# Fused attention and gated feed-forward: six single PSUM banks for the slots of batches 2 to 7

## The chip, the cores and the metric

The kernel runs on one core of a Trainium2 chip. The metric is the device time of one execution in microseconds (us). The names in the text: PE is TensorE (matrix products, and the weight loads PEld ahead of them), DVE is VectorE, ACT is ScalarE, POOL is GpSimd, SP is SyncE, which issues transfers. A bank is one of the eight pieces of PSUM, the memory that PE writes to; a bank holds 512 fp32 numbers in each of 128 partitions.

## The reference

```
def sm_attn(qq, kk, vv):
    s = scale * qq @ kk.T                  # per batch and head
    a = exp(s - max(s)); a = a / (sum(a) + 1e-9)
    return a @ vv
p_packed = sm_attn(p, k, v)                # 32 packed rows per head
out = sm_attn(q, p_packed, p_packed)       # 576 tokens per head
x = out as [8 * 576 tokens, 8 heads * 64]
h = x @ w_in                               # 512 -> 2048
g = h * cos(h)
result = g @ w_out                         # 2048 -> 512, fp32
```

There are 8 batches, 8 heads, 576 tokens, head size 64; the feed-forward part has 4608 rows, 512 inputs and 2048 hidden columns.

## The kernel before, in words

Everything is bf16 on PE, with fp32 in PSUM. The order on every engine is the order in which the code is written (`manual_schedule`); buffers only decide which earlier instruction a new one must wait for.

The second attention's product and w_in are merged: `ppw` multiplies the packed rows with w_in once per batch (PPW, in four quarters n = 0 to 3 of 512 columns), and h is then a2n (the normalised second attention weights, 256 rows in two halves y = 0, 1, 576 tokens) times PPW. The stages of batch s:

- `s2(s)`: 16 score products (L143) from ppT and q; ACT takes their exponentials into a2u.
- `sums2(s, y)`: PE sums each half with a block of ones (L239); ACT takes the logarithm (L241).
- `normalise(s)`: ACT takes exp(-log) for both halves (L247), then DVE multiplies a2u, the reciprocal of the first sums and that into a2n, first half 0, then half 1 (L249).
- `slot(s)`: 16 steps fc = 0 to 15, one for each 128 hidden columns. `h_mm` makes h for all 576 tokens in a pair of banks, 288 columns in each: two products with half 0 of a2n and two with half 1 (L263). ACT takes the cosine (L267, a sine with a bias), DVE the product h * cos(h) into gT (L270). After steps 7 and 15 POOL copies the last 64 tokens of eight steps into `joint` (L274), where two batches share 128 rows.
- Inside the slot, after step 7, `tiled` runs `ppw` quarters 2 and 3 (L213) and the packed rows `pp` of the next batch (L186), which are written into columns that h leaves unused in step 7's second bank (`spare`). After step 15's products `pp_T` (L198) transposes the packed rows of the next batch.

PE's gaps are filled with output products: `out_gen` gives, one at a time, the 128x512 products g @ w_out of the batch before (L351; 4 or 5 chunks of 16, accumulated in the two banks of the pool O, copied out by ACT or DVE and stored by SP), and `fill(n)` issues n of them. `slot` spreads those left over its steps, except for `keep`, which are left for later; `heavy={7: (5, 4)}` gives step 7 more, the last 4 of them behind its hook.

Besides O's two banks there are six. `banks(pairs)` closes the pool and opens it anew: `banks(3)` has three pairs (`psa`), `banks(0)` six single banks (`one`). Batch 0 runs its h with single banks, 512 tokens at a time (`h_one`), and its last 64 tokens follow in batch 1's slot at once (`h_rest`, L303); from batch 1 on there are three pairs.

PE's order in the stage of batch 4 (S scores, p8 the eight products of one `ppw`, Z the two of `sums2`, o an output product, H4 the four of a step, pp and T those of `pp` and `pp_T`):

```
S16 p8 o8 S16(first scores of batch 5) p8 o4 Z2 o5 Z2 o13
H4 o1 H4 o2 H4 o2 H4 o2 H4 o1 H4 o2 H4 o2 H4 o6 p16 pp48 o4
H4 o2 H4 o2 H4 o2 H4 o1 H4 o2 H4 o2 H4 o2 H4 T2 o7
```

Of the kernel before, what the change touches and what calls it, by code (L numbers as in the profile page):

```python
# [9 lines left out]
BF16 = mybir.dt.bfloat16  # L10
# [5 lines left out]
def kernel(  # L16
# [90 lines left out]
    def pe_T(n, b, engs=(V, V, V), groups=(0, 1, 2), own=None):  # L107
        if 0 in groups:
            xT[n, b] = att_pool.tile([128, H * 3, TP], BF16, name=n + "T", tag=n + "T", bufs=2 if n == "k" else 1)
        t = xT[n, b]  # L110
        flat = bf[n, b].rearrange("p h x -> p (h x)")
        for i in groups:
            ps = own(BF16) if own else psa(BF16)[:, 0, :]
            for j in range(8):
                o = 8 * i + j
                nc.tensor.transpose(ps[:, j * TP:(j + 1) * TP], flat[:, o * 128:(o + 1) * 128],  # L116
                                    ident[0:TP, 0:TP])
            to = t[:, 8 * i:8 * i + 8].rearrange("p a x -> p (a x)"), ps[:, 0:8 * TP]
            if engs[i] is None:
                return to  # L120
            copy(engs[i], *to)

    def bank(dt=FP32):
        return O.tile([128, 512 if dt == FP32 else 1024], dt, name="ot", tag="ot")
# [54 lines left out]
    def pp(b, eng=V, own=None):  # L179

        ps = own() if own else psa()[:, 0, :]
        for y in range(2):
            for j in range(C):
                c = 2 * (j % 3) + j // 3
                for x in range(4):
                    nc.tensor.matmul(ps[32 * x:32 * x + 32, y * D:(y + 1) * D],  # L186
                                     a1T[b][0:TP, y, j, 32 * x:32 * x + 32],
                                     bf["v", b][:, 2 * x + y, c * D:(c + 1) * D],
                                     start=(j == 0), stop=(j == C - 1))
        t = pp_sb[b % 2].rearrange("p a d -> p (a d)")  # L190
        copy(eng, t[:, 0:2 * D], ps[:, 0:2 * D])
        copy(eng, t[:, 2 * D:3 * D], ps[:, 0:D])
# [5 lines left out]
            nc.tensor.transpose(ps[:, i * 128:(i + 1) * 128], t[:, i * D:i * D + 128], ident)  # L198
        copy(eng, ppT[b % 2].rearrange("p i x n -> p (i x n)"), ps[:, 0:256])

    def ppw(b, n, eng=None, own=False, later=False, cuts=((0, 512),)):
        if b not in PPW:
            PPW[b] = ppw_pool.tile([128, 2, DF], BF16, name="PPW", tag="PPW")
        two = isinstance(eng, tuple)
        if own:
            ps = [bank(), bank()]
        else:
            t = psa()
            ps = [t[:, 0, :], t[:, 1, :]]
        for x in range(4):  # L210
            for y in range(2):
                r = slice(64 * y, 64 * y + 64)
                nc.tensor.matmul(ps[y][32 * x:32 * x + 32, :], ppT[b % 2][r, 0, x, :],  # L213
                                 w_in_bf[r, x, n * 512:(n + 1) * 512], start=True, stop=True)

        def evacuate(cuts=cuts):
            if own or two:
                for a, z in cuts:
                    for y in range(2):
                        copy(eng[y] if two else eng, PPW[b][:, y, n * 512 + a:n * 512 + z], ps[y][:, a:z])  # L220
            else:
                copy(eng or (V, ACT)[n % 2], PPW[b][:, :, n * 512:(n + 1) * 512], t)
        if later:
            return [lambda c=c: evacuate((c,)) for c in cuts]
        evacuate()
# [25 lines left out]

    gT, joint = {}, {}

    spare = [None]

    def h_mm(b, fc):
        if fc == 0:
            g_tile(b)
        ps = psa()
        spare[0] = ps[:, 1, HS:512]  # L260
        for y in range(2):
            for e in range(2):
                nc.tensor.matmul(ps[:, e, 0:HS], PPW[b][:, y, fc * 128:(fc + 1) * 128],  # L263
                                 a2n[b][:, y, e * HS:(e + 1) * HS], start=(y == 0), stop=(y == 1))
        cs = cos_pool.tile([128, S], BF16, name="cosT")
        csv = cs.rearrange("p (e x) -> p e x", e=2)
        ACT.activation(out=csv, in_=ps[:, :, 0:HS], func=AF.Sin, bias=PI_HALF)  # L267

        def rest():
            V.tensor_tensor(out=gT[b][:, fc, :].rearrange("p (e x) -> p e x", e=2),  # L270
                            in0=ps[:, :, 0:HS], in1=csv, op=ALU.mult)
            if fc % 8 == 7:
                j0 = (b % 2) * 64
                G.tensor_copy(out=joint[b // 2][:, fc - 7:fc + 1, j0:j0 + 64],  # L274
                              in_=gT[b][:, fc - 7:fc + 1, 512:576])
        return rest
# [21 lines left out]
    def h_rest(b):  # L298

        t = psa()  # L300
        for fc in range(NFC):
            for y in range(2):
                nc.tensor.matmul(t[:, fc // 8, (fc % 8) * 64:(fc % 8) * 64 + 64],  # L303
                                 PPW[b][:, y, fc * 128:(fc + 1) * 128], a2n[b][:, y, 512:576],
                                 start=(y == 0), stop=(y == 1))
        cs = cos_pool.tile([128, 2, 512], BF16, name="cosR", bufs=1)
        ACT.activation(out=cs, in_=t, func=AF.Sin, bias=PI_HALF)
        j0 = (b % 2) * 64
        V.tensor_tensor(out=joint[b // 2][:, :, j0:j0 + 64],
                        in0=t.rearrange("p a (f x) -> p (a f) x", x=64),  # L310
                        in1=cs.rearrange("p a (f x) -> p (a f) x", x=64), op=ALU.mult)

    osb_eng = [V]

# [50 lines left out]
    def to_do():  # L365
        return sum(n for _, n in filler)
# [73 lines left out]
    normalise(0)  # L440
    s1(1)
    ACT.preload_act_table_set(SIN_SET)
    cut_ppw, rest_ppw = ppw(0, 0, V, own=True, later=True, cuts=((0, 128), (128, 512)))
    warm(3, psa()[:, 0, :])
    cut_ppw()
    rest_ppw()
# [3 lines left out]
    for fc in range(13):  # L450
        h_one(0, fc)()()
        if fc in (0, 4, 8):
            ppw(0, 1 + fc // 4, (ACT, ACT if fc == 8 else V), own=True)
    c13 = h_one(0, 13)
    pp(1, ACT, own=bank)
    c13()()
# [27 lines left out]
    rest_ppw()  # L484
    fill(7)

    def slot(s, hooks, keep=0, heavy={}, last=None):


        left = to_do() - keep  # L490
        weight = [1 + heavy.get(fc, (0, 0))[0] for fc in range(NFC)]
        for fc in range(NFC):
            rest = h_mm(s, fc)
            if fc == NFC - 1 and last:
                last()
            rest()
            quota = (left * sum(weight[:fc + 1])) // sum(weight) - (left + keep - to_do())
            behind = min(quota, heavy[fc][1]) if fc in heavy else quota
            fill(quota - behind)
            while hooks and hooks[0][0] == fc:  # L500
                hooks.pop(0)[1]()
            fill(behind)
# [5 lines left out]
    def tiled(b):  # L508


        own, later = spare[0], []
        for n in (2, 3):
            later += ppw(b, n, (ACT, V)[n - 2], later=True)
        later[0]()
        pp(b + 1, V, own=lambda: own)
        later[1]()

    def tk2():
# [8 lines left out]
    def cross(n, b):  # L527
        return lambda: xbar(n, b)

    osb_eng[0] = ACT  # L530
    slot(1, [(2, lambda: pw2(1, 2, (ACT, V))), (4, lambda: h_rest(0)), (6, lambda: pack_p(2, 4)), (7, cross("k", 3)),
             (8, tk2), (9, cross("q", 2)), (10, lambda: pe_T("k", 2, (V, V, ACT), (2,)))], 4, {2: (1, 2), 4: (3, 5)})
    ACT.preload_act_table_set(EXP_SET)
    osb_eng[0] = V
    behind(xT["q", 2][0:1, 0, 0:1])
# [36 lines left out]
        load(n, b)  # L572
    fill(9)
    osb_eng[0] = ACT
    slot(2, [(7, lambda: tiled(2))], 10, {7: (5, 4)}, lambda: pp_T(3, V))

    for s in range(3, B):
        nxt = s + 1 < B
        ACT.preload_act_table_set(EXP_SET)
        osb_eng[0] = V  # L580
        set_filler(s - 1)
        fill(5)
        s2(s)
        ppw(s, 0, V)
        fill(8 if nxt else 9)
        if nxt:
            s1(s + 1)
            ppw(s, 1, V)
            a1_xbar(s + 1)
            xbar("q", s + 1)  # L590
            recips(s + 1)
            if s + 2 < B:
                xbar("k", s + 2)
                behind(xT["k", s + 2][0:1, 0, 0:1])
        else:
            for n in range(1, 4):
                ppw(s, n, V)
        fill(4 if nxt else 5)
        sums2(s, 0)
        fill(5)  # L600
        sums2(s, 1)
        normalise(s)
        ACT.preload_act_table_set(SIN_SET)
        fill(13)
        osb_eng[0] = ACT
        for n, b in (("v", s + 2), ("q", s + 2), ("k", s + 3)):
            if b < B:
                load(n, b)
        if nxt:
            slot(s, [(7, lambda: tiled(s))], 5 if s % 2 else 13, {7: (5, 4)}, lambda: pp_T(s + 1, V))  # L610
        else:
            slot(s, [], 5)
    set_filler(B - 1)
# [32 lines left out]
```

## Time and profile before

| | |
|---|---|
| median of 3 runs | 245.1 us (245.08 to 245.36) |
| the profiled execution | 245.1 us; its span, first to last instruction, 243.3 us; granted clock of PE 0.997 |
| PE | busy 233.8 us, 96% of the span |
| ACT, DVE, POOL | busy 166.1, 162.0 and 37.4 us |
| output products L351 | 560 of 128x512, about 380 ns each from start to end, one every 0.216 us back to back |
| step products L263 | 448 of 128x288, 286 ns each |
| cosine L267, product L270 | 112 each of 128x576, 652 and 757 ns each |
| chain that ended last | PE 82%, DVE 6%, ACT 1% of the span |

Products overlap: the next begins before the one before has ended, so their durations add up to more than the time that they take. Lines of the timeline give the start, the time from the first start to the last end, the engine, the line, what is written and read, and the count; in brackets stands how long the engine was idle before, and what ended that.

### The profile page before, as it was taken

To read this page: it belongs to the slowest core of one execution; us is meant where nothing else is said; L and a number is where in the kernel's file an instruction comes from. 1 tells how busy PE (TensorE), PEld (TensorE's weight loads), DVE (VectorE), ACT (ScalarE), POOL (GpSimd) and SP (SyncE) were. 2 spreads that over 40 slices of the span, in tenths; PEclk is the share of its full clock that TensorE was granted. 3 is DMA by queue.
4 is the path that set the end of the run, shared out by engine and by line. 5 is a ranking of instruction groups with operands and counts; after the bars stand their busy time and mean duration, and the time that the engine had idled before them with its cause. 6 is when DMAs were issued, how large, how long until landed. Compare 5 with 4: busy or idle time off the path is not lost.

```text
span 243.3 us, 5484 instructions
## 1 busy us (share of the span) xinstructions
PE 233.8 (96%) x2251; PEld 128.9 (53%) x2251; DVE 162.0 (67%) x256; ACT 166.1 (68%) x267; POOL 37.4 (15%) x60
## 2 busy tenths in 40 slices
PE   7789899999999999999999999999999999999994
PEld 3454354566446564556455654655455645665453
DVE  3259997787568795778758675868667878784001
ACT  2349999778478696868787687858796666773110
POOL 8432230210400041004100510030101010011000
PEclk9999999999999999999999999999999999999998
DMA  6999999999799999997999899999292111311133
GB/s 94 203 205 206 204 206 229 199 237 187 163 184 183 219 179 180 197 197 163 158 199 219 162 221 204 188 164 176 66 192 52 31 46 43 86 36 53 46 84 86
DMA packets 64377, 37.37 MB, mean 154 GB/s; under 512 B 36865, under 2 KB 59777, under 8 KB 64353
## 3 DMA queue, kind: packets, MB, share of 16 engines
q0 software_dynamic: 23152, 18.75, 51.0%
q1 hardware_dynamic: 40960, 18.16, 35.9%
q8 instruction: 17, 0.28, 0.4%
q10 hardware_dynamic: 240, 0.13, 0.2%
q14 instruction: 8, 0.06, 0.1%
HBM read 37.22 MB, written 9.44 MB: 192 GB/s over the span
## 4 chain that ended last, share of the span: by engine, by line
PE 82%; DVE 6%; ACT 1%; issue 1%; ACTq 0%
PE ot L351 50%; PE psA L263 22%; DVE gT L295 3%; PE psA L213 3%; PE psA L143 2%; PE psA L239 2%; PE ot L337 1%; PE psA L186 1%; DVE gT L270 1%; DVE PPW L87 1%; ACT cosT L267 1%; ACT cosT L294 0%; PE psA L116 0%; DVE qT L87 0%; PE psA L303 0%
## 5 line engine op out<-in xcount | busy, mean ns | idle before, releaser
L351 PE MATMUL ot<-w_out_bf,gT 128*128 128x512 bf16 x512 | 134.0, 379 | 0.0
L270 DVE TENSOR_TENSOR gT<-psA,cosT 128x576 bf16<-128x576 f32 x112 | 83.3, 757 | 21.0 <-ACT cosT L267 19.9
L267 ACT ACTIVATE cosT<-psA 128x576 bf16<-128x576 f32 x112 | 72.9, 652 | 24.9 <-PE psA L263 23.5
L263 PE MATMUL psA<-a2n,PPW 128*128 128x288 bf16 x448 | 73.3, 286 | 0.0
L351 PEld LDWEIGHTS <-gT 128*128 128x128 bf16 x512 | 48.2, 98 | 39.5 <-issue 4.2
L263 PEld LDWEIGHTS <-PPW 128*128 128x128 bf16 x448 | 43.8, 98 | 30.1 <-issue 0.4
L87 DVE CAST PPW<-psA 128x1024 bf16<-128x1024 f32 (+1 forms) x24 | 26.8, 1131 | 6.4 <-PE psA L213 6.2
L85 ACT COPY osb<-ot 128x512 f32<-128x512 f32 (+1 forms) x23 | 13.1, 569 | 16.2 <-PE ot L351 13.9
L87 DVE COPY osb<-ot 128x512 f32<-128x512 f32 (+2 forms) x15 | 9.7, 645 | 20.4 <-PE ot L337 17.2
L274 POOL COPY joint<-gT 128x512 bf16<-128x512 bf16 x14 | 8.6, 618 | 78.2 <-DVE gT L270 78.2
L249 DVE SCALAR_TENSOR_TENSOR a2n<-a2u,r,lns 128x576 bf16<-128x576 bf16 x16 | 12.4, 814 | 9.6 <-ACT lns L247 9.6
L152 ACT ACTIVATE a<-psA 128x576 bf16<-128x576 f32 x16 | 10.2, 646 | 8.2 <-PE psA L143 8.2
L241 ACT ACTIVATE lns<-psA 128x576 f32<-128x576 f32 x16 | 10.3, 650 | 7.2 <-PE psA L239 6.7
L351 PE MATMUL ot<-w_out_bf,joint 128*128 128x512 bf16 x48 | 12.2, 380 | 0.0
L98 POOL COPY gate<-kT 1x1 bf16<-1x1 bf16 x4 | 0.7, 180 | 72.7 <-DMA kT<-kbf 72.7
L231 ACT ACTIVATE a2u<-psA,rs 128x576 bf16<-128x576 f32 x16 | 11.0, 737 | 1.1 <-PE psA L143 1.0
L247 ACT ACTIVATE lns<-lns 128x576 f32<-128x576 f32 x16 | 10.0, 673 | 0.0
L213 PE MATMUL psA<-w_in_bf,ppT 64*32 64x512 bf16 x224 | 9.8, 379 | 0.0
L295 DVE TENSOR_TENSOR gT<-psH,cosT 128x512 bf16<-128x512 f32 x15 | 9.3, 680 | 0.4 <-ACT cosT L294 0.4
L391 PE MATMUL ot<-wz 128*128 128x512 f32 (+2 forms) x13 | 7.5, 661 | 1.9 <-DVE wz L404 1.7
L294 ACT ACTIVATE cosT<-psH 128x512 bf16<-128x512 f32 x15 | 8.4, 628 | 0.7 <-DVE gT L295 0.4
L289 PE MATMUL psH<-a2n,PPW 128*128 128x512 bf16 x30 | 7.8, 381 | 0.8 <-DVE PPW L87 0.8
(88 smaller groups left out, 170.6 us busy)
## 6 DMA issues: line engine op xcount, KB each, us to landing
kbf<-in_k_dram POOLq DMA_DIRECT2D x8, 576.0 KB, 14.0
vbf<-in_v_dram POOLq DMA_DIRECT2D x8, 576.0 KB, 7.8
qbf<-in_q_dram POOLq DMA_DIRECT2D x8, 576.0 KB, 10.9
out_dram<-osb SPq DMA_DIRECT2D x24, 192.0 KB, 2.6
out_dram<-osb SPq DMA_DIRECT2D x22, 128.0 KB, 2.9
w_in_bf<-in_moe_w_in_dram POOLq DMA_DIRECT2D x4, 512.0 KB, 17.3
w_out_bf<-in_moe_w_out_dram POOLq DMA_DIRECT2D x4, 512.0 KB, 20.8
out_dram<-osb SPq DMA_DIRECT2D x25, 64.0 KB, 2.3
```

The source lines that it names most:

```text
L85: ACT.copy(out=out, in_=in_)
L87: eng.tensor_copy(out=out, in_=in_)
L152: ACT.activation(out=a1[b % 2][:, y, :, 0:TP].rearrange("p (e m) x -> p e m x", e=2), in_=ps[y][:, :, 0:HS].rearrange("p e (m x) -> p e m ...
L213: nc.tensor.matmul(ps[y][32 * x:32 * x + 32, :], ppT[b % 2][r, 0, x, :], w_in_bf[r, x, n * 512:(n + 1) * 512], start=True, stop=True)
L231: ACT.activation(out=a2u[b][:, y].rearrange("p (e x) -> p e x", e=2), in_=ps[y][:, :, 0:HS], func=AF.Exp, scale=rs1[b][:, y:y + 1])
L241: ACT.activation(out=lns[b][:, y].rearrange("p (e x) -> p e x", e=2), in_=ps[:, :, 0:HS], func=AF.Ln)
L249: V.scalar_tensor_tensor(out=a2n[b][:, y], in0=a2u[b][:, y], scalar=r1[b][:, y:y + 1], in1=lns[b][:, y], op0=ALU.mult, op1=ALU.mult)
L263: nc.tensor.matmul(ps[:, e, 0:HS], PPW[b][:, y, fc * 128:(fc + 1) * 128], a2n[b][:, y, e * HS:(e + 1) * HS], start=(y == 0), stop=(y == 1))
L267: ACT.activation(out=csv, in_=ps[:, :, 0:HS], func=AF.Sin, bias=PI_HALF)
L270: V.tensor_tensor(out=gT[b][:, fc, :].rearrange("p (e x) -> p e x", e=2), in0=ps[:, :, 0:HS], in1=csv, op=ALU.mult)
L295: return lambda: V.tensor_tensor(out=gT[b][:, fc, 0:512], in0=ps, in1=cs, op=ALU.mult)
L351: nc.tensor.matmul(pss[c], w, w_out_bf[:, fc, :], start=(fc == 0), stop=(fc == NFC - 1))
```

## The change

From batch 2 on, `slot` opens six single banks (`banks(0)`) and makes each step with `h_one`: two products of 512 tokens, a cosine and a product of 512. The last 64 tokens come in two halves of eight steps (`h_rest_half`, 16 products of 64 columns each into one bank), as hooks after steps 5 and 11, and go straight into `joint`, so POOL's copies fall away there. `ppw` quarters 2 and 3, `pp` and `pp_T` take single banks (`one`), so one evacuation of 1024 columns becomes two of 512. At the end of a slot `banks(3)` returns to pairs. The scores of batches 3 to 7 come one output product later (`fill(6)` for `fill(5)`), and the slot follows one output product sooner after `sums2` (`fill(12)` for `fill(13)`); the `keep` of every slot but the last is one more. In slot 2, step 7 has one output product more, and 3 behind its hook instead of 4. Slot 1 stays with pairs. Batch 4 then runs:

```
S16 p8 o8 S16 p8 o4 Z2 o5 Z2 o12
h2 o1 h2 o2 h2 o2 h2 o2 h2 o1 h2 R16 o2 h2 o2 h2 o6 p16 pp48 o4
h2 o2 h2 o2 h2 o2 h2 R16 o1 h2 o2 h2 o2 h2 o2 h2 T2 o8
```

```diff
-    def ppw(b, n, eng=None, own=False, later=False, cuts=((0, 512),)):
+    def ppw(b, n, eng=None, own=None, later=False, cuts=((0, 512),)):
...
-            ps = [bank(), bank()]
+            ps = [own(), own()]
...
-        spare[0] = ps[:, 1, HS:512]
...
+    def h_rest_half(b, i):
+
+        t = one()
+        for j in range(8):
+            fc = 8 * i + j
+            for y in range(2):
+                nc.tensor.matmul(t[:, j * 64:(j + 1) * 64], PPW[b][:, y, fc * 128:(fc + 1) * 128],
+                                 a2n[b][:, y, 512:576], start=(y == 0), stop=(y == 1))
+        cs = cos_pool.tile([128, 512], BF16, name="cosT")
+        ACT.activation(out=cs, in_=t, func=AF.Sin, bias=PI_HALF)
+        j0 = (b % 2) * 64
+        V.tensor_tensor(out=joint[b // 2][:, 8 * i:8 * i + 8, j0:j0 + 64],
+                        in0=t.rearrange("p (f x) -> p f x", x=64),
+                        in1=cs.rearrange("p (f x) -> p f x", x=64), op=ALU.mult)
...
-    def slot(s, hooks, keep=0, heavy={}, last=None):
+    def slot(s, hooks, keep=0, heavy={}, last=None, single=True):
+        if single:
+            banks(0)
+            hooks = sorted(hooks + [(5, lambda: h_rest_half(s, 0)), (11, lambda: h_rest_half(s, 1))],
+                           key=lambda hook: hook[0])
...
-            rest = h_mm(s, fc)
+            rest = h_one(s, fc)() if single else h_mm(s, fc)
...
-        own, later = spare[0], []
+        later = []
         for n in (2, 3):
-            later += ppw(b, n, (ACT, V)[n - 2], later=True)
+            later += ppw(b, n, (ACT, V)[n - 2], own=one, later=True)
         later[0]()
-        pp(b + 1, V, own=lambda: own)
+        pp(b + 1, V, own=one)
...
-    slot(2, [(7, lambda: tiled(2))], 10, {7: (5, 4)}, lambda: pp_T(3, V))
+    slot(2, [(7, lambda: tiled(2))], 11, {7: (6, 3)}, lambda: pp_T(3, V, own=one))
...
+        banks(3)
...
-        fill(5)
+        fill(6)
         s2(s)
...
-        fill(13)
+        fill(12)
...
-            slot(s, [(7, lambda: tiled(s))], 5 if s % 2 else 13, {7: (5, 4)}, lambda: pp_T(s + 1, V))
+            slot(s, [(7, lambda: tiled(s))], 6 if s % 2 else 14, {7: (5, 4)}, lambda: pp_T(s + 1, V, own=one))
```

More of the change, by code (lines that the diff above doesn't have):

```diff
@@ L252 @@
     gT, joint = {}, {}
-    spare = [None]
     def h_mm(b, fc):
@@ L442 @@
     ACT.preload_act_table_set(SIN_SET)
-    cut_ppw, rest_ppw = ppw(0, 0, V, own=True, later=True, cuts=((0, 128), (128, 512)))
+    cut_ppw, rest_ppw = ppw(0, 0, V, own=bank, later=True, cuts=((0, 128), (128, 512)))
     warm(3, psa()[:, 0, :])
@@ L452 @@
         if fc in (0, 4, 8):
-            ppw(0, 1 + fc // 4, (ACT, ACT if fc == 8 else V), own=True)
+            ppw(0, 1 + fc // 4, (ACT, ACT if fc == 8 else V), own=bank)
     c13 = h_one(0, 13)
@@ L531 @@
     slot(1, [(2, lambda: pw2(1, 2, (ACT, V))), (4, lambda: h_rest(0)), (6, lambda: pack_p(2, 4)), (7, cross("k", 3)),
-             (8, tk2), (9, cross("q", 2)), (10, lambda: pe_T("k", 2, (V, V, ACT), (2,)))], 4, {2: (1, 2), 4: (3, 5)})
+             (8, tk2), (9, cross("q", 2)), (10, lambda: pe_T("k", 2, (V, V, ACT), (2,)))], 4, {2: (1, 2), 4: (3, 5)}, None, False)
     ACT.preload_act_table_set(EXP_SET)
```

## The prediction

> **What bounds the kernel now.** I read the page's busy rows first, then TensorE's (PE's) own waits from 74 to 222 us (batches 2 to 7, where the change lies), then the timeline where a slot begins, where the pooled products (`tiled`) run, and where a slot ends. The profiled execution took 245.1 us, which is also the median of the three runs; its span is 243.3 us, so 1.8 us lie outside it and stay.
>
> ```profile
> PE 233.8 (96%) x2251; PEld 128.9 (53%) x2251; DVE 162.0 (67%) x256; ACT 166.1 (68%) x267; POOL 37.4 (15%) x60
> ```
>
> ```profile
> PE psA L186 <- DVE gT L270: 0.2, 1, 0.2
> ```
>
> PE has work without a break (the page's clock row reads 9 to the last slice), and the only wait of PE for another engine that the view of 148 us counts is 0.2 us long, once (the columns are the total, the times, the longest). So PE's stream sets the end: what the change is worth is what it takes from or adds to that stream, and the waits that it ends or makes.
>
> **The arithmetic of h on PE.** A step of `h_mm` is four products of 288 columns, a step of `h_one` two of 512, and the last 64 tokens cost two products of 64 per step. Slot 7 runs steps back to back with output products (chain of waits, 205.5 to 222 us), and the 64-column form ran once, in slot 1 (timeline):
>
> ```profile
> 205.93 0.49 PE psA L263 x4
> 206.42 0.43 PE ot L351 x2
> 206.85 0.49 PE psA L263 x4
> ```
>
> ```profile
> 46.79 1.10 PE L303 MATMUL psA<-a2n,PPW 128*128 128x64 bf16 x32
> 47.72 1.24 PE L351 MATMUL ot<-w_out_bf,gT 128*128 128x512 bf16 x5
> ```
>
> Five steps from 205.93 to 210.54 take 4.61 us, 0.922 each. A product of 512 columns takes 0.216 (13 of them in 2.81 us before slot 4), so the four of 288 take 0.922 - 0.432 = 0.490. The new step: 2 x 0.216 = 0.432, plus 2 x 0.0291 (32 in 47.72 - 46.79 = 0.93 us) = 0.058, together 0.490 to 0.491. Over 6 slots of 16 steps that is 0 to +0.1 us. I take +0.05; the columns are the same 1152, only cut otherwise.
>
> A rule speaks against the small products. The Trainium skill ("TensorE: Matmul & The Clock Gate", Back-to-back issue gap) says that in a stream of weight loads and matmuls the spacing is set by both, about 81 ns a matmul at 128 columns; by that the 192 new small products would cost, as an estimate, 192 x (81 - 29) = 10 us more. The 32 products above came every 29 ns with a weight load each, so the sum goes by the row.
>
> **What waits end.** In `tiled`, `pp` (L186) borrows the unused columns of step 7's bank, so it must wait until DVE has made step 7's product. Slot 2 (timeline; start, duration):
>
> ```profile
> 81.34 0.63 PE L213 MATMUL psA<-w_in_bf,ppT 64*32 64x512 bf16 x16
> ...
> 82.15 0.55 PE L186 MATMUL psA<-vbf,a1T 96*32 96x64 bf16 x48 [0.18 <-DVE gT L270]
> ```
>
> From first to first it is 0.81 us here and 0.55 in slots 3 to 6 (107.37 to 107.92 in slot 3): 0.25 us of waiting, in slot 2 alone. With six banks a slot takes 24 of them in turn (16 steps, 2 halves, 4 for `ppw`, 1 for `pp`, 1 for `pp_T`), and `pp` gets the bank of step 6, long drained. At the slot's end `pp_T` (L198) takes the third pair back, and needs step 13's product:
>
> ```profile
> 89.09 0.65 PE L263 MATMUL psA<-a2n,PPW 128*128 128x288 bf16 x4
> ...
> 89.72 0.27 PE L198 MATMUL psA<-ident,pp_sb 128*128 128x128 bf16 x2
> ```
>
> Four products take 0.49, so it could start at 89.58 and starts 0.14 later; in slot 3 (115.09, 115.65) 0.07 later, after that not at all. In the changed kernel its bank was step 11's. So 0.25 + 0.14 + 0.07 = 0.46 us end. That is all that more banks can bring, since there are no other waits.
>
> **The wait that grows.** `fill(5)` becomes `fill(6)` ahead of the scores and `fill(13)` becomes `fill(12)` between `sums2(s, 1)` and the slot, s = 3 to 7. PE's work is the same in sum, but the slot now begins one output product, 0.216 us, sooner after `sums2(s, 1)`, and from there hangs the chain that makes a2n. Slot 6 (timeline):
>
> ```profile
> 175.58 0.41 PE L239 MATMUL psA<-a2u,ones_blk 128*128 128x288 bf16 x2
> ...
> 175.83 2.97 PE L351 MATMUL ot<-w_out_bf,gT 128*128 128x512 bf16 x13
> 176.03 0.65 ACT L241 ACTIVATE lns<-psA 128x576 f32<-128x576 f32 x1 [0.67 <-PE psA L239]
> ...
> 176.57 1.25 ACT L247 ACTIVATE lns<-lns 128x576 f32<-128x576 f32 x2
> 177.28 1.55 DVE L249 SCALAR_TENSOR_TENSOR a2n<-a2u,r,lns 128x576 bf16<-128x576 bf16 x2 [1.02 <-ACT lns L247]
> ...
> 178.63 0.66 PE L263 MATMUL psA<-a2n,PPW 128*128 128x288 bf16 x4
> ```
>
> The logarithm starts when PE is done, each link starts on the heels of the one before, and DVE ends at 178.83. Step 0's third product, the first to read the second half of a2n, begins at 178.63 + 0.245 = 178.88. It is just in time: there is no slack. That this wait is real shows in slot 1, where it is too early and four products take 0.86 instead of 0.65 us:
>
> ```profile
> 39.09 1.55 DVE L249 SCALAR_TENSOR_TENSOR a2n<-a2u,r,lns 128x576 bf16<-128x576 bf16 x2 [1.81 <-ACT lns L247]
> ...
> 40.23 0.86 PE L263 MATMUL psA<-a2n,PPW 128*128 128x288 bf16 x4
> ```
>
> After the change step 0 starts at 178.63 - 0.216 = 178.41, and its second product already reads the second half: due at 178.63, possible at 178.88. The stall is 0.25 us in each of slots 3 to 7. In slot 2 `fill(9)` stays and only the second reason holds: due 74.30 + 0.216 = 74.52, possible at 74.55, 0.03 us. Together 5 x 0.25 + 0.03 = 1.28 us. Bounds: if PE needed no time at all after DVE's end, 0.20 each, 1.0 us; if the chain ran later by the 0.05 us by which slots differ, 1.5 us. Queued behind the waiting product is everything on PE, all output products included.
>
> **What lies beside other work.** ACT and DVE make 18 passes of 512 per slot instead of 16 of 576. DVE's 512 pass comes every 0.60 us (four in 2.39 us at 24.71), its 576 pass every 0.66 to 0.70: 10.8 against some 11. ACT's take 628 against 652 ns. A `ppw` evacuation is two of 0.68 us instead of one of 1.22 on DVE, and 2 x 0.59 against 1.01 on ACT. A slot lasts 17 us of PE, and in the 27 us of batch 5 DVE waits 2.8 and ACT 3.7 us for h's own links, so this costs nothing; uncovered it would be 0.1 to 0.3 us a slot. The 12 POOL copies of the last 64 tokens (0.62 us each) go; nobody waits for them, and POOL's loads hang on the gate copy (72.7 us waiting for a transposed k), which stays. SP's stores move by one output product. Scores and the transpose of a1 come 0.22 us later within the stage; `pp` reads a1 at 134.07 in slot 4, 8.7 us after its transpose has been issued (121.56 + 3.79).
>
> The handover of banks at a slot's end: the scores get the banks of half 2 and steps 12 to 14, and `ppw(s, 0)` those of step 15 and `pp_T`. Step 15's product ended at 143.91 before (143.15 + 0.76), and `ppw` started at 144.12, now 144.34. No wait, as long as DVE isn't 0.4 us later.
>
> Sum: +0.05 - 0.46 + 1.28 = +0.87 us, so 245.1 + 0.9 = 246.0 us, or 0.36% slower. A measurement of this kernel tells about 0.2%, 0.5 us, from no change.
>
> **The rivals.**
> - Only half of the stall appears, because the chain to a2n gets shorter on freer ACT and DVE: 5 x 0.12 + 0.03 - 0.46 + 0.05 = +0.2, 245.3 us. Against: every link of the chain in slot 6 starts as soon as the one before allows, so there is no queue to shorten. 0.13, with smaller shortfalls.
> - Faster. The 0.55 us from `ppw` to `pp` are not 16 products' worth; some 0.30 us pass after the last. If that pause is a bank wait, `pp`'s own bank ends it in slots 2 to 6: -1.5 us, so 244.5. It decides from 0.28 us each. Against: from the scores' `ppw` to the next output product, which needs no new bank, the same 0.3 us pass (from 144.12 to 144.46). 0.06. The Trainium skill ("Perfetto Trace Analysis", Matmul Optimizations) asks to use all eight banks for the sake of overlap; by the waits above that rule has 0.46 us to give here.
> - Slower still. If DVE trails by one pass (0.60 us) at the slot's end, because of the half at step 11, `ppw(s, 0)` waits for step 15's bank until 144.51 + 0.05, 0.22 us in each of five slots: 247.1 us. For: ACT and DVE get three passes in a row there. Against: four steps of 0.92 us follow, each with only 0.6 us of DVE. 0.10.
> - The weight loads of the small products aren't hidden: 98 ns (the load's row) instead of 29, times 192, 13 us: 259 us. The 32 products in slot 1 speak against it. 0.01.
>
> **How the numbers follow.** My forecast has 0.70, with 245.6 to 246.5 as its own range (stall 1.0 to 1.5 us, arithmetic 0 to 0.1, and 0.1 for the spread of runs). With the half stall the range is 245.3 to 246.7. Faster by over 0.2%: 0.06; within: 0.13 and a little of the forecast's low end, 0.14; slower: the rest, 0.80.
>
> **What would show it.** In the changed profile: step 0 of slots 3 to 7 with 0.25 us between its two products beyond 0.216, its releaser DVE's a2n; `ppw` to `pp` 0.55 us in slot 2 too; no gap ahead of `pp_T`; halves of 0.46 us each; 16 steps at 0.43. It is wrong if PE doesn't wait at the slots' starts, or waits where the banks change hands.

## The result and the profile after

The changed kernel takes 246.06 us (median of 9 runs, 245.75 to 247.7), the kernel before, measured beside it, 245.08 (9 runs, 244.98 to 245.36). The ratio on record is 1.0047, with a 95% interval of 1.003 to 1.0064; the quotient of the two medians is 1.0040. One run of the changed kernel, 247.7 us at a granted clock of 1.0, lies apart from the other eight (up to 246.33), and why is open. The prediction said 246.0 us, range 245.3 to 246.7, slower.

The page's busy and chain rows answer least here:

```profile
PE 231.5 (95%) x2216; PEld 115.4 (47%) x2251; DVE 163.0 (67%) x273; ACT 167.2 (69%) x284; POOL 30.1 (12%) x48
...
PE 77%; DVE 8%; ACT 3%; issue 2%; DVEq 0%; ACTq 0%
PE ot L363 44%; PE psH L286 17%; DVE gT L292 3%; PE psA L260 3%; DVE a2n L249 3%; PE psH L316 2%; PE psA L143 2%; PE psA L213 2%; PE psA L239 2%; PE ot L349 1%; ACT lns L241 1%; ACT lns L247 1%; PE psH L213 1%; PE psH L186 1%; DVE PPW L87 1%
```

ACT's and DVE's busy time moved by about 1 us, POOL's twelve copies are gone. PE is less busy in a longer run, but of 2251 products 35 have no record here (all 2251 weight loads have one), so its busy time can't be compared. Still, the chain says where to look: PE fell from 82 to 77% of it, DVE rose from 6 to 8 and ACT from 1 to 3, and a2n (L249) stands in it with 3%, where the chain of before had no line of it among its largest fifteen. (In this kernel L363 is the output product, L286 the step's, L316 the half's, L291 the cosine, L292 DVE's product.)

PE's own waits from 74 to 224 us (total, times, longest) show nothing of the kind:

```profile
PE ot L363 <- issue: 1.6, 10, 0.2
```

That is all there is, and these ten gaps of 0.16 us stand where the record of one output product is missing. This view counts idle time between one product's end and the next one's start; a product lasts 0.38 us while the next is due 0.216 after its start, so up to 0.16 us of every wait lies inside the product before it. The readings below go by starts instead. Slot 6 begins like this (timeline; start, time from first start to last end):

```profile
175.65 0.41 PE L239 MATMUL psA<-a2u,ones_blk 128*128 128x288 bf16 x2
...
175.89 2.75 PE L363 MATMUL ot<-w_out_bf,gT 128*128 128x512 bf16 x12
...
176.64 1.25 ACT L247 ACTIVATE lns<-lns 128x576 f32<-128x576 f32 x2
177.35 1.55 DVE L249 SCALAR_TENSOR_TENSOR a2n<-a2u,r,lns 128x576 bf16<-128x576 bf16 x2 [1.02 <-ACT lns L247]
...
178.48 0.84 PE L286 MATMUL psH<-a2n,PPW 128*128 128x512 bf16 x2
...
179.38 0.59 PE L286 MATMUL psH<-a2n,PPW 128*128 128x512 bf16 x2
```

DVE ends a2n at 177.35 + 1.55 = 178.90. Step 0's two products take 0.84 us from first start to last end, step 1's 0.59: the second product comes 0.25 us late, at 178.48 + 0.84 - 0.38 = 178.94. The same 0.25 stands in slots 3 to 7, 0.03 in slot 2; in all six the second product starts 0.05 us after DVE's end.

The prediction's other signs, in slot 2: `ppw` to `pp` is 81.88 - 81.33 = 0.55 us, and there is no gap ahead of `pp_T`, which starts 0.43 us, two products, after step 15's first:

```profile
81.33 0.63 PE L213 MATMUL psH<-w_in_bf,ppT 64*32 64x512 bf16 x16
81.88 0.56 PE L186 MATMUL psH<-vbf,a1T 96*32 96x64 bf16 x48
...
88.46 0.59 PE L286 MATMUL psH<-a2n,PPW 128*128 128x512 bf16 x2
...
88.89 0.28 PE L198 MATMUL psH<-ident,pp_sb 128*128 128x128 bf16 x2
```

Each half (`h_rest_half`, 16 products) takes 0.47 us (chain that ended last, 178 to 200 us, the two halves of slot 6):

```profile
183.21 0.47 PE psH L316 x16
...
191.73 0.47 PE psH L316 x16
```

To leave out what happens in the prologue, I compare kernels from the first product of slot 2 to the first product of the tail, by the starts in the trace: 161.75 us before (74.30 to 236.05), 162.56 after (74.05 to 236.60). So +0.81, the 1.28 of the stall less the 0.46 of the waits, and nothing for the arithmetic. Each stretch is read from one trace, and it repeats well where two programs are alike: the kernel before and that of experiment 5 take 136.37 us each from the first product of slot 3 on, the changed kernel and that of experiment 6, which from slot 4 on differ only in banks that PE doesn't wait for, 111.64 us each from there. All experiments are read in this stretch too:

| kernel | median, us (runs) | ratio to before, interval | stretch, us | from the kernel that it starts from |
|---|---|---|---|---|
| before | 245.08 (9) | | 161.75 | |
| after | 246.06 (9) | 1.0047 (1.003 to 1.0064) | 162.56 | +0.81 |
| after, move undone | 245.19 (12) | 0.9999 (0.998 to 1.0018) | 161.55 | -1.01 |
| before, move alone | 246.37 (12) | 1.0031 (1.0012 to 1.0051) | 162.82 | +1.07 |
| after, move twice | 247.06 (6) | 1.007 (1.0043 to 1.0098) | 163.64 | +1.08 |
| after, first halves ahead | 245.16 (12) | 0.9992 (0.9977 to 1.0007) | 161.45 | -1.11 |
| before, six and three | 245.0 (1) | one run | 161.72 | -0.03 |
| after, old banks | 247.03 (1) | one run | 163.01 | +0.45 |
| after, first halves, slot later | 244.86 (12) | 0.9977 (0.9959 to 0.9996) | 161.30 | -1.26 |
| after, first halves, move undone | 244.85 (12) | 0.9971 (0.9952 to 0.999) | 161.37 | -1.19 |

The kernel before had a median of 245.23 us (29 runs) beside the first four experiments and 245.34 (23 runs) beside the others; the ratios are to these. They are those on record, not quotients of the medians, and can differ from such a quotient by up to 0.0015 (1.0046 for the move alone).

### The profile page after: what moved, and what is told of

Its sections match the earlier page's. It is cut to its first block, busy times and chain, and to the rows that moved or that the text cites. A ratio compares the mean times of both kernels' runs of the same rounds, so it can differ in the third digit from the quotient of the medians.

```text
span 243.8 us, 5472 instructions
## 1 busy us (share of the span) xinstructions
PE 231.5 (95%) x2216; PEld 115.4 (47%) x2251; DVE 163.0 (67%) x273; ACT 167.2 (69%) x284; POOL 30.1 (12%) x48
## 4 chain that ended last, share of the span: by engine, by line
PE 77%; DVE 8%; ACT 3%; issue 2%; DVEq 0%; ACTq 0%
PE ot L363 44%; PE psH L286 17%; DVE gT L292 3%; PE psA L260 3%; DVE a2n L249 3%; PE psH L316 2%; PE psA L143 2%; PE psA L213 2%; PE psA L239 2%; PE ot L349 1%; ACT lns L241 1%; ACT lns L247 1%; PE psH L213 1%; PE psH L186 1%; DVE PPW L87 1%
## 5 line engine op out<-in xcount | busy, mean ns | idle before, releaser
L363 PE MATMUL ot<-w_out_bf,gT 128*128 128x512 bf16 x486 | 129.4, 379 | 2.6 <-issue 1.9
L292 DVE TENSOR_TENSOR gT<-psH,cosT 128x512 bf16<-128x512 f32 x111 | 74.7, 689 | 15.9 <-ACT cosT L291 15.0
L291 ACT ACTIVATE cosT<-psH 128x512 bf16<-128x512 f32 x111 | 65.8, 603 | 19.1 <-PE psH L286 16.4
L363 PEld LDWEIGHTS <-gT 128*128 128x128 bf16 x512 | 47.7, 98 | 53.1 <-issue 6.3
L286 PE MATMUL psH<-a2n,PPW 128*128 128x512 bf16 x219 | 65.0, 379 | 1.5 <-DVE PPW L87 0.8
L286 PEld LDWEIGHTS <-PPW 128*128 128x128 bf16 x224 | 21.4, 98 | 27.1 <-DVE PPW L87 1.8
L87 DVE CAST PPW<-psA 128x1024 bf16<-128x1024 f32 (+1 forms) x19 | 20.7, 1110 | 7.2 <-PE psA L213 7.0
L249 DVE SCALAR_TENSOR_TENSOR a2n<-a2u,r,lns 128x576 bf16<-128x576 bf16 x16 | 12.4, 815 | 9.6 <-ACT lns L247 9.6
L267 DVE TENSOR_TENSOR gT<-psA,cosT 128x576 bf16<-128x576 f32 x16 | 12.0, 757 | 3.1 <-ACT cosT L264 3.1
L264 ACT ACTIVATE cosT<-psA 128x576 bf16<-128x576 f32 x16 | 10.4, 653 | 3.8 <-PE psA L260 3.5
L363 PE MATMUL ot<-w_out_bf,joint 128*128 128x512 bf16 x45 | 11.7, 380 | 0.2
L260 PE MATMUL psA<-a2n,PPW 128*128 128x288 bf16 x64 | 10.5, 286 | 0.0
L85 ACT CAST PPW<-psH 128x512 bf16<-128x512 f32 x10 | 5.4, 589 | 5.1 <-PE psH L213 5.1
L316 PEld LDWEIGHTS <-PPW 128*128 128x128 bf16 x192 | 7.2, 98 | 2.8
```

Of the source, the lines that this page charges most:

```text
L85: ACT.copy(out=out, in_=in_)
L87: eng.tensor_copy(out=out, in_=in_)
L249: V.scalar_tensor_tensor(out=a2n[b][:, y], in0=a2u[b][:, y], scalar=r1[b][:, y:y + 1], in1=lns[b][:, y], op0=ALU.mult, op1=ALU.mult)
L286: nc.tensor.matmul(ps, PPW[b][:, y, fc * 128:(fc + 1) * 128], a2n[b][:, y, 0:512], start=(y == 0), stop=(y == 1))
L291: ACT.activation(out=cs, in_=ps, func=AF.Sin, bias=PI_HALF)
L292: return lambda: V.tensor_tensor(out=gT[b][:, fc, 0:512], in0=ps, in1=cs, op=ALU.mult)
```

## The experiments

### 1. The move undone in the changed kernel

```diff
-        fill(6)
+        fill(5)
         s2(s)
...
-        fill(12)
+        fill(13)
...
-            slot(s, [(7, lambda: tiled(s))], 6 if s % 2 else 14, ...
+            slot(s, [(7, lambda: tiled(s))], 5 if s % 2 else 13, ...
```

> The changed kernel with the output products back where they were: five ahead of the scores, thirteen ahead of the slot, keep one less. Theory (the slot starts too early for the second half of a2n): step 0 of slots 3 to 7 starts 0.216 us later against the a2n chain, its second product waits 0.03 us instead of 0.25, so 5 x 0.216 = 1.1 us go: 246.06 - 1.08 = 245.0 us, and nothing waits at the scores. Rival A (the scores were moved because the banks change hands too late): a wait of up to 0.22 us appears at the scores or at ppw(s, 0) in each stage, and the time stays at 245.8 to 246.1. Rival B (the loss lies in the h products of 512 and 64 columns): 246.0 us.

Measured: 245.19 us, not to be told from before; the stretch is 1.01 us shorter than after's. Step 0 of slot 6 (timeline of PE) now takes 0.62 us instead of 0.84:

```profile
178.67 0.62 PE L286 MATMUL psH<-a2n,PPW 128*128 128x512 bf16 x2
...
179.35 0.59 PE L286 MATMUL psH<-a2n,PPW 128*128 128x512 bf16 x2
```

In all six slots the second product comes 0.247 to 0.250 us after the first, 0.03 late, as in slot 2 of the changed kernel. So the moved output product carries the loss; a loss in the arithmetic or in the banks as such would have stayed. The sum holds here too: -0.46 of waits, 6 x 0.03 of stall and 0.07 for a new wait make -0.21 against before, and the stretch has 161.55 - 161.75 = -0.20. The 0.07 is the handover of the banks, here with five output products between slot 2 and the scores (timeline):

```profile
90.49 0.68 DVE L292 TENSOR_TENSOR gT<-psH,cosT 128x512 bf16<-128x512 f32 x1
...
91.22 0.14 PEld L143 LDWEIGHTS <-ppT 64*32 64x32 bf16 x16 [0.49 <-DVE gT L292]
```

The scores' first weight load starts 0.05 us after DVE's product of step 15 has ended (91.17). In the changed kernel, one output product later, DVE ends at 89.94 + 0.68 = 90.62 and the load starts at 90.82, 0.20 after it:

```profile
89.94 0.68 DVE L292 TENSOR_TENSOR gT<-psH,cosT 128x512 bf16<-128x512 f32 x1
...
90.82 0.14 PEld L143 LDWEIGHTS <-ppT 64*32 64x32 bf16 x16 [0.42 <-DVE gT L292]
```

### 2. The move alone in the kernel before

```diff
-        fill(5)
+        fill(6)
...
-        fill(13)
+        fill(12)
...
-            slot(s, [(7, lambda: tiled(s))], 5 if s % 2 else 13, ...
+            slot(s, [(7, lambda: tiled(s))], 6 if s % 2 else 14, ...
```

> The kernel before, with pairs of banks, and only the move: six output products ahead of the scores, twelve ahead of the slot, keep one more, for batches 3 to 7. Theory: the third product of step 0 (the first on the second half of a2n) comes 0.216 us sooner and waits 0.22 us in each of five slots, 245.08 + 1.1 = 246.2 us; the 0.46 us of waits at pp and pp_T stay. Rivals A and B: there is nothing of the new banks or of the new products in it, so 245.1 us.

Measured: 246.37 us, 1.0031; the stretch is 1.07 us longer. With pairs too, step 0 waits for a2n; its third product comes 0.343 us after the second, instead of the 0.12 at which two such products follow each other without a wait (timeline of PE, slot 6; step 0 takes 0.87, step 1 0.65):

```profile
179.41 0.87 PE L263 MATMUL psA<-a2n,PPW 128*128 128x288 bf16 x4
...
180.33 0.65 PE L263 MATMUL psA<-a2n,PPW 128*128 128x288 bf16 x4
```

Five stalls of 0.22 make 1.10. The move alone costs this much, whatever the banks. With single banks each stall is 0.03 longer, as the second half is read by the second of two products, 0.216 after the first, not by the third of four, 0.245 after it.

### 3. The move made twice

```diff
-        fill(6)
+        fill(7)
...
-        fill(12)
+        fill(11)
...
-            slot(s, [(7, lambda: tiled(s))], 6 if s % 2 else 14, ...
+            slot(s, [(7, lambda: tiled(s))], 7 if s % 2 else 15, ...
```

> The changed kernel with the move made once more: seven output products ahead of the scores, eleven ahead of the slot, keep one more again. Theory: the wait of step 0's second product grows by one output product, 0.25 to 0.47 us in each of slots 3 to 7: 246.06 + 1.08 = 247.1 us. If the wait has another cause than the distance from sums2 to the slot, it stays at 0.25 and the time at 246.1.

Measured: 247.06 us, 1.007; the stretch is 1.08 us longer than after's, 5 x 0.216. The second product of step 0 comes 0.68 us after the first, and now the wait is long enough for the view of waits (74 to 224 us) to name it, less the 0.16 us that lie inside the first product:

```profile
PE psH L286 <- DVE a2n L249: 1.5, 5, 0.3
```

So each output product taken from between `sums2` and the slot comes back in full as stall: a2n is due at a fixed time after `sums2(s, 1)`, and PE has nothing else that it may do first.

### 4. First halves first

```diff
+    def h_half(b, fc, ps, y):
+        nc.tensor.matmul(ps, PPW[b][:, y, fc * 128:(fc + 1) * 128], a2n[b][:, y, 0:512], ...
-    def h_one(b, fc, own=None):
+    def h_one(b, fc, own=None, pair=False):
...
+            h_half(b, fc, ps, 0)
+            if pair:
+                ahead[b, fc + 1] = one()
+                h_half(b, fc + 1, ahead[b, fc + 1], 0)
+        h_half(b, fc, ps, 1)
...
-            rest = h_one(s, fc)() if single else h_mm(s, fc)
+            rest = h_one(s, fc, pair=fc == 0)() if single else h_mm(s, fc)
```

The products of steps 0 and 1 with the first half of a2n come first, then step 0's with the second half; step 1's second product follows in its place. Nothing else changes, `fill(6)` and `fill(12)` included.

> The changed kernel, the output products as changed, but in each slot of batches 2 to 7 PE makes the first-half product of step 0 and then that of step 1 before the second halves of both. Theory: the second half of a2n is needed 0.432 us after the slot's start instead of 0.216, the waits fall from 0.25 to 0.03 us in slots 3 to 7 and to none in slot 2: 246.06 - 1.1 = 244.9 to 245.0 us, the same as undoing the move. If the wait is not for the second half of a2n but for the first, or for a bank, it stays and the time is 246.1.

Measured: 245.16 us, 0.9992; the stretch is 1.11 us shorter than after's. The first product with the second half is now the third (timeline of PE, slot 6), 178.28 + 0.84 - 0.38 = 178.74, two products and 0.03 after the first:

```profile
178.28 0.84 PE L283 MATMUL psH<-a2n,PPW 128*128 128x512 bf16 x3
```

Without the move being undone, one product that doesn't need the late half takes the place of the stall. That names the cause closely: PE waits for the second half of a2n, not for a bank, a2n as a whole or the shifted scores. Of the 1.28 us, 5 x 0.03 = 0.15 are left.

### 5. Before, with six output products and three behind in slot 2

The prediction had put the 0.25 us ahead of `pp` down to its bank. But the change also puts one more output product ahead of `ppw` in slot 2. Two runs tell these apart; here only the products move.

```diff
-    slot(2, [(7, lambda: tiled(2))], 10, {7: (5, 4)}, lambda: pp_T(3, V))
+    slot(2, [(7, lambda: tiled(2))], 10, {7: (6, 3)}, lambda: pp_T(3, V))
```

> The kernel before, with pairs, and of the change only slot 2's heavy={7: (6, 3)}: one output product more ahead of the ppw and pp of slot 2, one fewer behind. Theory A (pp's own bank ended the 0.25 us of waiting in slot 2): with pairs pp still borrows step 7's bank, so the wait stays, 0.81 us from ppw's first product to pp's first. Theory B (the shift ended it): pp comes 0.216 us later against step 7's product, and 0.56 to 0.60 us is seen. In both the gaps ahead of pp_T stay, 0.14 and 0.07 us or a little more. The time can't tell them apart (245.0 to 245.2).

Measured: one run of 245.0 us; the stretch is 0.03 us shorter. `ppw` to `pp` is 0.55 us, with the old bank (timeline of PE):

```profile
81.70 0.63 PE L213 MATMUL psA<-w_in_bf,ppT 64*32 64x512 bf16 x16
82.25 0.56 PE L186 MATMUL psA<-vbf,a1T 96*32 96x64 bf16 x48
...
88.56 0.38 PE L351 MATMUL ot<-w_out_bf,joint 128*128 128x512 bf16 x1
88.95 0.65 PE L263 MATMUL psA<-a2n,PPW 128*128 128x288 bf16 x4
89.61 0.27 PE L198 MATMUL psA<-ident,pp_sb 128*128 128x128 bf16 x2
```

So the shifted output product ends that wait by itself. Yet the time is hardly won: PE, 0.25 us further on, meets the banks later in the slot, and DVE has not moved along: its product of step 13 ends 15.36 us after the slot's first product in the kernel before and 15.33 here. Step 15's products start 0.39 us after the output product ahead of them instead of 0.216 (they take the bank pair of step 12), and `pp_T` still starts 0.17 late (89.61 against 88.95 + 0.49).

### 6. After, with the old banks

`pp` in step 7's bank and `pp_T` in step 13's, as with pairs; all else as in the changed kernel.

```diff
-        ps = (own or one)()
+        ps = held[fc] = (own or one)()
...
-        pp(b + 1, V, own=one)
+        pp(b + 1, V, own=lambda: held[7])
...
+    def third_back(dt):
+        return held[13].bitcast(dt)
...
-    slot(2, ..., lambda: pp_T(3, V, own=one))
+    slot(2, ..., lambda: pp_T(3, V, own=third_back))
...
-            slot(s, ..., lambda: pp_T(s + 1, V, own=one))
+            slot(s, ..., lambda: pp_T(s + 1, V, own=third_back))
```

> The changed kernel, but pp writes into step 7's bank once that product is made, and pp_T into step 13's, as with the pairs. Theory A (their own banks ended the 0.46 us of waits): in slot 2 some 0.25 us ahead of pp and 0.14 or more ahead of pp_T, in slot 3 0.07 ahead of pp_T, come back, and the time rises by 0.5 us to 246.5. Theory B (for pp the shifted output product did it): no more than 0.03 us ahead of pp, and only the gaps ahead of pp_T come back, 0.2 to 0.5 us in all.

Measured: one run of 247.03 us (its slot 2 began 0.8 us later than after's, so the time says little); the stretch is 0.45 us longer than after's. `pp` still doesn't wait (timeline of PE); `pp_T` does, in slot 2 by 90.09 - 89.27 - 0.43 = 0.39 us and in slot 3 by 0.06:

```profile
82.14 0.63 PE L213 MATMUL psH<-w_in_bf,ppT 64*32 64x512 bf16 x16
82.69 0.56 PE L186 MATMUL psH<-vbf,a1T 96*32 96x64 bf16 x48
...
89.27 0.59 PE L286 MATMUL psH<-a2n,PPW 128*128 128x512 bf16 x2
...
90.09 0.27 PE L198 MATMUL psH<-ident,pp_sb 128*128 128x128 bf16 x2 [0.23 <-DVE gT L292]
```

Together 0.45, the stretch's own difference. So the extra banks are worth about what the prediction gave them, 0.46, but at another place: `pp` gains nothing from its bank, `pp_T` has all of it. DVE's product of step 13 ends 15.19 us after the slot's first product here as in the changed kernel; so in slot 2 a PE that is let go earlier meets DVE at the next bank that it needs back.

### 7 and 8. Two versions without the stall

With first halves first, the 0.03 us left in each slot and the output product's place can still be chosen. One version puts `fill(13)` ahead of the slot and leaves the scores behind `fill(6)`, so that the slot has one output product less:

```diff
-        fill(12)
+        fill(13)
```

> The changed kernel with both mendings where neither costs: the first-half products of steps 0 and 1 ahead of the second halves, scores behind six output products as changed, and thirteen instead of twelve ahead of the slot (the slot has one fewer). Theory: no wait is left on PE from slot 2 on, since the second half of a2n is then needed 0.65 us after where the changed kernel's slot began: 246.06 - 1.28 = 244.8 us, and from slot 2's first product to the tail 161.3 us (before 161.75, changed 162.56). If other costs of single banks were hidden behind the stall, they come out now and it is not faster than the kernel before.

The other has the edits of experiments 1 and 4 together:

> The changed kernel with the first-half products of steps 0 and 1 ahead and the output products back at five ahead of the scores and thirteen ahead of the slot. Theory: no stall for a2n in any slot, 246.06 - 1.28 + 0.07 = 244.85 us; the 0.07 us is a wait of the first scores after slot 2 for step 15's product, as in the first experiment, since all six banks change hands at once. If the scores don't wait, 244.8.

Measured: 244.86 us (0.9977, interval 0.9959 to 0.9996) and 244.85 us (0.9971, 0.9952 to 0.999). Both are ahead of both kernels, by 0.5 us of the kernel before; which of them is better the runs don't tell. In the first, no wait of PE is left in the six slots: step 0 of slot 6 takes three products' time and no more (timeline of PE; two spacings of 0.216 and one product of 0.38 make 0.81),

```profile
178.15 0.81 PE L283 MATMUL psH<-a2n,PPW 128*128 128x512 bf16 x3
```

and its stretch, 161.30, is 0.45 under before's: the 0.46 of the change's own gain, which the stall had covered. The second keeps the 0.07 us ahead of the scores after slot 2 (161.37).

## Why the prediction was right, point by point

- **The arithmetic of h**, 0 to +0.1, taken as +0.05. Measured at nothing: 16 small products take 0.47 us, 29 ns each, and the stretch's +0.81 is 1.28 - 0.46 with 0.01 left over. The weight loads of the small products, 98 ns each, stay hidden. The Trainium skill ("TensorE: Matmul & The Clock Gate", Back-to-back issue gap) has about 81 ns for a load and a matmul in a stream at 128 columns. The 192 small products here have 64 columns and a load each and come nowhere near that, so the measured 29 ns decide.
- **The stall of a2n**, 1.28. Right in place, size and count: 0.25 in slots 3 to 7, 0.03 in slot 2. Experiments 1 to 4 show the cause from both sides: the move alone makes it, the move undone ends it, the move twice adds 0.216 to each, and a product that needs only the first half fills it. What the prediction could lean on was that the chain in slot 6 of before had each link on the heels of the one before, so that "just in time" meant no slack at all.
- **The waits that end**, 0.46. The sum was right, one step was not: "`pp` gets the bank of step 6, long drained" was given as what ends the 0.25 us. Experiment 5 has that wait end with the old bank, by the one output product that the change puts ahead of `ppw`; the prediction's diff shows it, and its sum did not count it as a shift. Experiment 6 has the banks' gain at `pp_T`, 0.39 and 0.06, not 0.14 and 0.07. The size came out right because a wait that is ended without a bank comes back at the next bank; the prediction didn't give that reason, so on this point its number was lucky. The Trainium skill ("Perfetto Trace Analysis", Matmul Optimizations) asks that all eight PSUM banks be used. Both kernels hold all eight, so that rule doesn't tell them apart; banks of their own for `pp` and `pp_T` gave 0.45 us in experiment 6.
- **The handover of banks.** The prediction had the scores take the banks of half 2 and steps 12 to 14 one at a time, with step 15's for `ppw(s, 0)`. The built program has the scores' first weight load wait for DVE's product of step 15 (experiment 1), which fits the pool being closed and opened anew, so that all six banks change hands at once. It cost nothing in the changed kernel, but the load came 0.20 us after DVE's end in slot 2, where 0.05 are needed: 0.15 us to spare, not the 0.4 that the prediction named. Where the scores come one output product sooner, as in experiment 1, it costs 0.07 us there.
- **What lies beside other work.** ACT and DVE still wait for h inside the slots (groups by line of the changed kernel, 150 to 177 us; total, mean ns, then idle time and its releaser):

```profile
L291 ACT ACTIVATE cosT<-psH 128x512 bf16<-128x512 f32 x16 | 9.6, 600 | 3.6 <-PE psH L286 3.3 <-DVE gT L292 0.2
...
L292 DVE TENSOR_TENSOR gT<-psH,cosT 128x512 bf16<-128x512 f32 x16 | 10.9, 691 | 2.5 <-ACT cosT L291 2.5
```

  So their two more passes a slot stay covered, as forecast.
- **The rivals.** Half a stall: every stall is whole. A shorter pause from `ppw` to `pp` because of the bank: it is 0.55 us with the new bank and with the old. DVE late at the slot's end: its last pass ends 0.2 to 0.4 us ahead of the scores' load in slots 2 to 6. Unhidden weight loads: 29 ns each.

The two kernels' profiled executions differ by only 245.75 - 245.1 = 0.65 us, less than the 0.81 of the stretch, as the changed kernel's prologue happened to be 0.25 us shorter (slot 2 begins at 74.05 against 74.30) and some 0.1 us more lie outside both. The medians of nine runs, 0.98 us apart, lie on the other side of it.

## What to carry to other kernels

When filler work is moved on the engine that sets the end, look at the chain that starts ahead of the place it is taken from: if its last link is just in time, every filler product taken from there comes back as a stall, whatever the same product does elsewhere. As good as giving the filler back is to order the waiting work by what arrives first (245.16 us in experiment 4, 245.19 in experiment 1): one product that needs only the early half removed nearly all of a stall of 0.25 us. And a wait that ends is not yet time won; before counting it, follow the engine to the next resource that it needs back from the same late partner.

## What the runs showed of the hardware that was not expected

The first transposes of k, which in nine of the ten profiles wait for the transfer that brings k, start at another time in each run (timeline of PE, before and after):

```profile
8.23 1.15 PE L116 MATMUL psA<-ident,kbf 96*128 96x96 bf16 x23 [1.14 <-DMA kbf<-in_k_dram]
```

```profile
7.96 1.19 PE L116 MATMUL psA<-ident,kbf 96*128 96x96 bf16 x24 [0.20 <-DMA kbf<-in_k_dram]
```

In the profiled runs of the ten kernels these starts lie between 7.88 and 8.56 us, and DVE's first a2n follows 11.23 to 11.25 us later in all of them. From there to the a2n of slot 1 it is 19.62 or 19.63 us in seven profiles, but 19.71, 19.90 and 20.08 in three others, and why is open. Slot 2 begins between 74.05 and 74.86, though the changes come later: as much as the whole effect studied here. A difference of 0.5 us is therefore read from a stretch of the trace first, and from medians of a dozen runs after that.
